# Block sums leave PSUM by another engine, a plain guard, the last store in pieces, and a new order: attention and a relu² network on one core

## The chip, the cores and the metric

The kernel runs on one core of a Trainium2 chip. Its engines have separate instruction queues: TensorE (PE) multiplies, VectorE (DVE), ScalarE (ACT) and GpSimd (POOL) do elementwise work, and SyncE (SP) issues the transfers (DMAs). SBUF is the memory on the chip that the engines work in; PSUM is the one that PE writes into and DVE and ACT can read. The metric is the device time of one execution, in microseconds; the median of three is shown. An engine works through its queue strictly in order, so an instruction that waits holds all behind it.

## What is computed

```python
k_sum = k.reshape(B, H, nb, 32, D).max(axis=3)        # B, H, S, D = 4, 8, 768, 64;  nb = 24
v_sum = v.reshape(B, H, nb, 32, D).mean(axis=3)
scores_l = scale * q @ k.T, masked to |i - j| < 16
scores_s = scale * q @ k_sum.T + log(32)
a = exp(scores - max);  a = a / (a.sum() + 1e-9)      # over both kinds of keys together
x = a @ concat(v, v_sum)                              # 3072 tokens x 512
r = maximum(x @ w_in, 0);  out = (r * r) @ w_out      # 512 -> 2048 -> 512
```

All is float32. Each query sees its neighbours within 15 places and one summary of each of the 24 blocks of its sequence.

## The kernel before

**Attention.** The queries are cut into 48 groups of 64; a group is all 8 heads of 64 positions, in four tiles of 128 rows (two heads each). A row of scores has 118 columns: 94 neighbours and 24 block summaries. Per group, in this order: PE makes the scores (L840; for the first eight groups the mask is added by a second matmul, whose left side is the constant `unscale`), DVE takes each row's maximum (L933) and scales it (L937), ACT takes the exps and sums them (L978), DVE adds 1e-9 to the sums (L990) and inverts them (L993), DVE multiplies the rows by the inverse (L999), PE transposes them (L1028), ACT copies the transposed tile out (L1035), and PE multiplies by the values (L1099) to give `att`, the x of the network. x is then split into a high part (`xh`, ACT L1156) and a rest (`xl`, DVE L1159), since PE multiplies at full rate only in a shorter format; each product of the network is the sum of three terms (high·high, high·rest, rest·high).

The mean values of the blocks of the first batch are made by PE (`vps`) and copied out of PSUM by the task `VS0` (L674): four copies of 24 rows and 128 columns into `fv_lent`. POOL copies them from there into the value tiles of the first eight groups (L795). The maxima of keys are taken by DVE (L595), four to a batch.

**The network.** 3072 tokens are six units of 512. The first two are done plainly: for each of 16 column blocks f of 128, `h` = x·w_in (L1296, twelve matmuls of 512 columns), relu, square and split (ACT L1305, L1306, L1309, DVE L1312), then `o` += g·w_out (L1322, twelve matmuls). The first two blocks of the first unit are done in halves of 256 tokens, called 0a, 1a, 0b, 1b, since only four groups are ready at first. The weights come as 64-bit words and are turned into high and rest by ACT (L1222, L1239) and DVE (L1225, L1231, L1246), one tile per block, in the time of the first unit. The other four units are done in two stages of products of sums of quarters (Strassen's scheme): L1837 and L1620 on PE. Of the last stage's last product the sums are added to `u` by DVE in two halves (L1566), each stored by a transfer (L1559).

**What sets the order.** Each piece of work is a task with an engine, a cost and a due time (`add` of the class `Plan`). `Plan.order` simulates the engines: whenever an engine comes free it takes the ready task with the earliest due time. The instructions of each engine are then issued in the order that it found. So the tables of due times (`SUMS_AT`, `VISITS`, `COMBS`, and `NUDGE`, which shifts single tasks) and the costs only set the order; the hardware runs each queue in that order, and waits by semaphores.

## Times and profile before

| | |
|---|---|
| median of 3 runs | 568.62 us (567.89, 568.62, 568.65) |
| profiled execution | 567.89 us |
| its span | 566.1 us (1.8 us lie around it) |
| PE busy | 556.9 us, 98% |
| DVE, ACT, POOL busy | 83%, 66%, 6% |
| chain that ended last | PE 93%, DVE 4%, DMA 1%, ACT 1% |
| granted clock of PE | full in all slices |

The span is the stretch that the profiler's trace covers. Busy is the time in which an engine runs something; the share of the whole span is an average over stages that have different limits, so the section of rows below cuts it into stretches. The chain is followed back from the last instruction, at each step to what released it. A row of the timeline has the idle time of its engine ahead of it in brackets, with what ended it.

### The profile page before, as it was taken

To read this page: it belongs to the slowest core of one execution; us is meant where nothing else is said; L and a number is where in the kernel's file an instruction comes from. 1 tells how busy PE (TensorE), PEld (TensorE's weight loads), DVE (VectorE), ACT (ScalarE), POOL (GpSimd) and SP (SyncE) were. 2 spreads that over 40 slices of the span, in tenths; PEclk is the share of its full clock that TensorE was granted. 3 is DMA by queue.
4 is the path that set the end of the run, shared out by engine and by line. 5 is a ranking of instruction groups with operands and counts; after the bars stand their busy time and mean duration, and the time that the engine had idled before them with its cause. 6 is when DMAs were issued, how large, how long until landed. Compare 5 with 4: busy or idle time off the path is not lost.

```text
span 566.1 us, 11857 instructions
## 1 busy us (share of the span) xinstructions
PE 556.9 (98%) x3952; PEld 458.7 (81%) x3952; DVE 471.0 (83%) x1190; ACT 373.9 (66%) x968; POOL 36.3 (6%) x88
## 2 busy tenths in 40 slices
PE   8899999999999999999999999999999999999996
PEld 7688888888888888888888888888888888888885
DVE  5999999989799998999978889997493466868863
ACT  3899799778877887786336688847375532554441
POOL 5400000012001130000000200000000000000000
PEclk9999999999999999999999999999999999999999
DMA  8998999999999999899877989897975677767682
GB/s 303 348 372 319 350 316 375 302 335 330 361 301 317 329 334 358 291 298 400 279 226 230 293 246 290 273 281 232 303 210 161 190 196 193 190 199 230 196 228 91
DMA packets 86810, 156.75 MB, mean 277 GB/s; under 512 B 8996, under 2 KB 30566, under 8 KB 86750
## 3 DMA queue, kind: packets, MB, share of 16 engines
q1 hardware_dynamic: 85597, 152.95, 83.2%
q0 software_dynamic: 1152, 3.05, 3.2%
q8 instruction: 32, 0.52, 0.4%
q14 instruction: 29, 0.23, 0.1%
HBM read 111.66 MB, written 47.94 MB: 282 GB/s over the span
## 4 chain that ended last, share of the span: by engine, by line
PE 93%; DVE 4%; DMA 1%; ACT 1%; SPq 0%; issue 0%; DVEq 0%
PE o L1620 23%; PE o L1322 16%; PE h L1296 15%; PE o L1837 14%; PE sz L1837 8%; PE x L1099 4%; PE att L1620 4%; PE att L840 3%; PE sa L1837 3%; PE att L1837 2%; DMA kb<-kT 1%; DVE small L933 1%; PE t L1028 1%; DVE qvpa_lent L999 1%; ACT qvpa_lent L978 1%; DVE kb L595 0%
## 5 line engine op out<-in xcount | busy, mean ns | idle before, releaser
L1602 ACT CAST gh<-g 128x512 fp32r<-128x512 f32 x112 | 69.2, 621 | 53.1 <-PE o L1620 22.7
L1620 PE MATMUL o<-gh,w 128*128 128x512 f32 x384 | 103.3, 391 | 0.0
L1607 DVE TENSOR_TENSOR gl<-g,gh 128x512 fp32r<-128x512 f32 x112 | 76.1, 686 | 21.1 <-ACT gh L1602 19.9
L1620 PEld LDWEIGHTS o<-gh,w 128*128 128x128 f32 x384 | 71.7, 188 | 15.0
L1296 PE MATMUL h<-xh,w 128*128 128x512 f32 x240 | 74.5, 392 | 0.0
L1874 ACT ACTIVATE g<-g 128x512 f32<-128x512 f32 x60 | 37.8, 632 | 49.4 <-DVE g L1870 49.3
L1322 PE MATMUL o<-w,gh 128*128 128x512 f32 x240 | 62.3, 396 | 0.0
L978 ACT ACTIVATE p<-p,small 128x118 f32<-128x118 f32 x160 | 61.5, 389 | 0.3 <-DVE small L915 0.2
L1620 PE MATMUL o<-gl,w 128*128 128x512 f32 x192 | 59.2, 390 | 0.0
L1296 PEld LDWEIGHTS h<-xh,w 128*128 128x128 f32 x240 | 44.7, 188 | 9.5 <-ACT rl_0b L1305 0.2
L1322 PEld LDWEIGHTS o<-w,gh 128*128 128x128 f32 x240 | 44.2, 188 | 9.3 <-ACT rl L1306 0.2
L1296 PE MATMUL h<-xl,w 128*128 128x512 f32 x120 | 46.8, 390 | 0.0
L1620 PEld LDWEIGHTS o<-gl,w 128*128 128x128 f32 x192 | 36.0, 188 | 7.5
L1837 PE MATMUL o<-w,w 128*128 128x512 f32 x160 | 40.5, 389 | 0.0
L1837 PEld LDWEIGHTS o<-w,w 128*128 128x128 f32 x160 | 30.0, 188 | 6.2
L915 DVE CUSTOM_DVE_ANT_0 p<-att,mask 128x118 f32<-128x118 f32 x152 | 33.0, 276 | 2.1 <-PE att L840 2.0
L1837 PE MATMUL sz<-xh,w 128*128 128x512 f32 x128 | 34.3, 390 | 0.0
L1322 PE MATMUL o<-w,gl 128*128 128x512 f32 x120 | 33.6, 390 | 0.0
L1597 DVE TENSOR_TENSOR g<-g 128x512 f32<-128x512 f32 x48 | 32.7, 686 | 0.2
L1870 DVE CUSTOM_DVE_ANT_0 g<-sz,g 128x512 f32<-128x512 f32 x32 | 22.0, 687 | 12.0 <-ACT g L1857 6.9
L978 ACT ACTIVATION_READ_ACCUMULATOR p<-p,small 128x1 f32 x160 | 30.8, 193 | 0.0
L1837 PE MATMUL o<-xh,w 128*128 128x512 f32 x112 | 30.1, 391 | 0.0
(197 smaller groups left out, 1092.3 us busy)
## 6 DMA issues: line engine op xcount, KB each, us to landing
raw<-wW SPq DMA_DIRECT2D x32, 512.0 KB, 8.1
w<-scr_t SPq DMA_DIRECT2D x64, 256.0 KB, 2.8
w<-scr_s SPq DMA_DIRECT2D x64, 256.0 KB, 3.1
w<-scr_a SPq DMA_DIRECT2D x48, 256.0 KB, 3.2
w<-scr_i SPq DMA_DIRECT2D x44, 256.0 KB, 3.1
turn<-a SPq DMA_DIRECT2D x17, 512.0 KB, 4.2
scr_t<-ci SPq DMA_DIRECT2D x16, 512.0 KB, 6.7
v<-vS SPq DMA_DIRECT2D x34, 192.0 KB, 3.4
```

What stands on the lines that cost most here:

```text
L915: nc.vector.tensor_tensor_reduce(out=pr.tile[:, j, :KEYS], in0=score_at(g, 0, j), in1=mask_of(g)[0], scale=-SCALE, scalar=-NEG, op0=ALU.ad ...
L978: nc.scalar.activation(x, score_tile(g, p % parts)[:, p] if by_pe else x, AF.Exp, bias=nm.tile[:, p : p + 1], scale=SCALE if by_pe else -1 ...
L1099: nc.tensor.matmul(x_of(i)[h % 2 * D : (h % 2 + 1) * D, h // 2, :], lhsT=v_bufs[g].tile[:KEYS, h * D : (h + 1) * D], rhs=av[:KEYS, 2 * c : ...
L1296: nc.tensor.matmul(cut(h), lhsT=lhs.tile[:, k // 2, k % 2 * P : (k % 2 + 1) * P], rhs=rhs[:, k, c0 : c0 + n], start=(i == 0), stop=(i == 3 ...
L1322: nc.tensor.matmul(o_of(o, t).rearrange("p (h c) -> p h c", h=2), lhsT=terms[i][0].tile[:, (t - t0) * P : (t - t0 + 1) * P], rhs=terms[i][ ...
L1597: lambda x=x, ins=ins, op=op: nc.vector.tensor_tensor(out=x.tile, in0=ins[0].tile, in1=ins[1].tile, op=op),
L1602: f"GH{s}_{n}", "ACT", 0.54, lambda x=x, gh=gh: nc.scalar.copy(out=gh.tile, in_=x.tile), due - GH_LEAD, ready,
L1607: lambda x=x, gh=gh, gl=gl: nc.vector.tensor_tensor(out=gl.tile, in0=x.tile, in1=gh.tile.bitcast(F32), op=ALU.subtract),
L1620: nc.tensor.matmul(o.tile[:, d], lhsT=chunk.tile[:, w * HALF + d * P : w * HALF + (d + 1) * P], rhs=y.tile, start=begins and w == 0 and y ...
L1837: nc.tensor.matmul(o.tile, lhsT=lhs(w, k), rhs=y[k], start=begins and i == 0, stop=i == 5, skip_group_check=not begins,)
L1870: lambda: nc.vector._custom_dve(TENSOR_ADD_SAT, out=to.tile, in0=o.tile, in1=x.tile, s0=HUGE, s1=0.0), key, deps,
L1874: f"G{name}_{s}", "ACT", 0.57, lambda: nc.scalar.activation(to.tile, to.tile, AF.Square), key + 0.7, [t], use=[to]
```

## The change

- The four copies of `VS0` are done by ACT in place of DVE.
- The guard (adding 1e-9) was a tensor-scalar instruction with two operations and an accumulator that is read by a second instruction; it is now one plain addition. The planner's cost for it is lower, and it counts it among the instructions that can hold or be held by POOL (`LOCKS`).
- The last product of all is made in three groups of matmuls: the first 128 rows of it whole, the other 128 by columns 0 to 255 and 256 to 511. Each has its own sum and its own store.
- The left side of the mask term is the identity matrix in place of `unscale`. The possibility to scale q ahead is added but not used (`Q_SCALED_BY` is eight dashes).
- The masks beyond the second are due later on POOL.
- All tables of due times are new, so every queue is in another order.

```diff
-FIRST_LS = -32.673
+FIRST_LS = -186.491
...
+FIRST_SUMS_BY = 'A'
...
-SUMS_AT = (50.909, 101.7, 156.402)
+SUMS_AT = (52.647, 93.76, 176.523)
...
-        d = at[1]
+        d, c = at[1], at[2] if len(at) > 2 else slice(None)
         if isinstance(d, int):
-            return self.bufs[d].tile
+            return self.bufs[d].tile[:, c]
         assert d.stop == d.start + 1
-        return self.bufs[d.start].tile.unsqueeze(1)
+        return self.bufs[d.start].tile[:, c].unsqueeze(1)
...
         def gather():
             for c in range(ns):
-                nc.vector.tensor_copy(out=vs.tile[:NB, c * DM // ns : (c + 1) * DM // ns], in_=out_ps.tile[c * SQ : c * SQ + NB, : DM // ns])
+                (nc.vector.tensor_copy if FIRST_SUMS_BY == "D" else nc.scalar.copy)(
+                    out=vs.tile[:NB, c * DM // ns : (c + 1) * DM // ns], in_=out_ps.tile[c * SQ : c * SQ + NB, : DM // ns]
+                )
...
-                            lhsT=q_bufs[g].tile[rows, p, :] if term else unscale[rows, :],
+                            lhsT=q_bufs[g].tile[rows, p, :] if term else unscale[rows, :] if g in t_QS else ident[rows, rows],
...
-        nm = buf("nm", 3, (P, 3 * NPAIR + 1), F32, f"nm{g}")
+        nm = buf("nm", 3, (P, 3 * NPAIR), F32, f"nm{g}")
...
-            nc.vector.tensor_scalar(
-                out=rec, in0=den, scalar1=1e-9, scalar2=0.0, op0=ALU.add, op1=ALU.add, accum_out=nm.tile[:, 3 * NPAIR : 3 * NPAIR + 1]
-            )
+            nc.vector.tensor_scalar_add(rec, den, 1e-9)
             nc.vector.reciprocal(out=rec, in_=rec)
...
-            for i, piece in enumerate((todo[::2], todo[1::2]) if end else (todo,)):
+            whole = slice(0, TU)
+            pieces = [(todo, whole)]
+            if end:
+                pieces = [(todo[::2], whole), (todo[1::2], slice(0, TU // 2)), (todo[1::2], slice(TU // 2, TU))]
+            for i, (piece, c) in enumerate(pieces):
...
-                    d = slice(i, i + 1)
-                    t = plus("C12", u2, o, u2, due + 2, [t_p, made["U2"]], d=d)
-                    leave(f"12_{s}_{i}", u2, 0, 1, due + 3, [t], d)
+                    d = slice(i > 0, 1 + (i > 0))
+                    t = plus("C12", u2, o, u2, due + 2 + 0.1 * i, [t_p, made["U2"]], d=d, c=c)
+                    leave(f"12_{s}_{i}", u2, 0, 1, due + 3 + 0.1 * i, [t], d, c)
```

The lines of the changed kernel have numbers up to 19 higher than those of before: L674 stays, L933 is L952, L937 is L956, L978 is L991, L990 is L1003, L999 is L1010, L1035 is L1046, L1296 is L1307, L1322 is L1333.

First place: DVE's queue where the copies of the block sums stood. `small` holds the maxima, sums and inverses of a group (three buffers in turn), `o` are scores in PSUM, `qvpa_lent` rows after the exps. Before:

```order
L999 TENSOR_TENSOR qvpa_lent<-qvpa_lent,small_85 128x4x118
L674 COPY fv_lent<-vps_325 24x128 x4
L990 TENSOR_SCALAR small_86<-small_86 128x4
L993 RECIPROCAL small_86<-small_86 128x4
L933 TENSOR_REDUCE small_72<-o_66 128x4
L937 TENSOR_SCALAR small_72<-small_72 128x4
```

The same place now:

```order
L1010 TENSOR_TENSOR qvpa_lent<-qvpa_lent,small_85 128x4x118
L952 TENSOR_REDUCE small_72<-o_66 128x4
L956 TENSOR_SCALAR small_72<-small_72 128x4
L1003 TENSOR_SCALAR small_86<-small_86 128x4
L1004 RECIPROCAL small_86<-small_86 128x4
L1010 TENSOR_TENSOR qvpa_lent<-qvpa_lent,small_86 128x4x118
```

The copies are gone, and the maximum of the next group (number 3) stands ahead of the guard.

Second place: ACT's queue at the exps of that group (`small_72`) and of the next. Before:

```order
L1035 COPY qvpa_lent<-t_421 128x4x4x32
L978 ACTIVATE qvpa_lent,small_72<-o_66,small_72 128x118 x4
L1035 COPY qvpa_lent<-t_456 128x4x4x32
L978 ACTIVATE qvpa_lent,small_85<-o_67,small_85 128x118 x4
L1156 CAST xh<-att_68 128x4x64
L1035 COPY qvpa_lent<-t_510 128x4x4x32
```

And now:

```order
L1046 COPY qvpa_lent<-t_406 128x4x4x32
L991 ACTIVATE qvpa_lent,small_72<-o_66,small_72 128x118 x4
L674 COPY fv_lent<-vps_323 24x128 x4
L1046 COPY qvpa_lent<-t_451 128x4x4x32
L991 ACTIVATE qvpa_lent,small_85<-o_67,small_85 128x118 x4
L1046 COPY qvpa_lent<-t_495 128x4x4x32
```

The four copies stand between the exps of the group and the copy of a transposed tile; the cast of x, which stood ahead of the last row, comes later.

Third place: PE's queue at the third column block, `h_2`. `gh_0a` and `gl_0a` are the high part and the rest of block 0 for the first half of the tokens, `gh_1a` and `gl_1a` those of block 1. Before:

```order
L1322 MATMUL o_67<-w_0_624,gh_0a 128x512 x2
L1322 MATMUL o_67<-w_0_624,gl_0a 128x512
L1296 MATMUL h_2_855<-xh,w_2_807 128x512 x2
L1296 MATMUL h_2_855<-xl,w_2_807 128x512
...
L1322 MATMUL o_67<-w_1_724,gh_1a 128x512 x4
L1322 MATMUL o_67<-w_1_724,gl_1a 128x512 x2
```

And now:

```order
L1333 MATMUL o_67<-w_1_704,gh_1a 128x512 x4
L1333 MATMUL o_67<-w_1_704,gl_1a 128x512 x2
L1307 MATMUL h_1b<-xh,w_1_716 128x256 x2
L1307 MATMUL h_1b<-xl,w_1_716 128x256
...
L1307 MATMUL h_2_870<-xh,w_2_829 128x512 x2
L1307 MATMUL h_2_870<-xl,w_2_829 128x512
```

The six matmuls of block 1's first half stood behind `h_2` and stand now ahead of it, and ahead of `h_1b` too.

## Rows read from the trace of the kernel before

**Rows 1.** Busy time by stretch: PE, PEld, DVE, ACT, POOL; PEclk, DMA share, GB/s

```profile
10.00:40.45 30.45, 27.23 (x532) 22.34 (x531) 28.57 (x93) 27.04 (x102) 7.87 (x23) 1.00 0.99 361
40.45:561.56 521.11, 521.11 (x3362) 428.30 (x3360) 437.52 (x1092) 344.55 (x863) 22.19 (x31) 1.00 0.87 274
561.56:566.10 4.54, 0.00 (x0) 0.00 (x0) 0.73 (x2) 0.00 (x0) 0.00 (x0) 0.94 0.32 116
```

**Rows 2.** Waits of PE: who, for whom, us in total, times, longest

```profile
PE t L1028 <- DVE qvpa_lent L999: 2.4, 4, 0.9
```

**Rows 3.** Chain of waits, 0 to 46 us: start, length, what

```profile
17.57 0.29 DVE fv_lent L674
...
19.06 1.47 ACT qvpa_lent L978 x8
...
20.88 1.51 ACT qvpa_lent L978 x8
```

**Rows 4.** Timeline of DVE, 14 to 26 us: start, length, instruction

```profile
16.69 1.17 DVE L674 COPY fv_lent<-vps 24x128 f32<-24x128 f32 x4
17.79 0.14 DVE L990 TENSOR_SCALAR_CACHE_REDUCE small<-small 128x4 f32<-128x4 f32 x1
...
18.86 0.17 DVE L937 TENSOR_SCALAR small<-small 128x4 f32<-128x4 f32 x1
...
20.17 0.46 DVE L937 TENSOR_SCALAR small<-small 128x4 f32<-128x4 f32 x1
```

**Rows 5.** Groups of ACT's instructions by form: busy us, mean ns | idle before

```profile
L1156 ACT CAST xh<-att 128x256 fp32r<-128x256 f32 x8 | 2.9, 387 | 0.0
L864 ACT COPY kw<-kb 128x96 f32<-128x96 f32 x19 | 5.3, 278 | 6.2 <-DVE kb L595 5.6 <-POOL kb L853 0.5
```

**Rows 6.** Timeline of ACT, 14 to 26 us

```profile
19.06 0.36 ACT L978 ACTIVATE qvpa_lent<-o,small 128x118 f32<-128x118 f32 x1 [0.64 <-DVE small L937]
...
22.88 0.58 ACT L1035 COPY qvpa_lent<-t 128x512 f32<-128x512 f32 x1 [0.24 <-PE t L1028]
```

**Rows 7.** Chain of waits, the second half product of block 1

```profile
44.83 1.36 PE o L1322 x6
```

**Rows 8.** Timeline of PE, 33 to 47 us

```profile
41.84 0.71 PE L1296 MATMUL h<-xh,w 128*128 128x512 f32 x2
```

**Rows 9.** Timeline of DVE, 38 to 78 us

```profile
41.10 0.66 DVE L1246 TENSOR_TENSOR w<-t,w 128x512 fp32r<-128x512 f32 x1
...
63.09 1.80 DVE L595 TENSOR_REDUCE kb<-kb 128x24 f32<-128x768 f32 x2
...
71.30 1.18 DVE L1246 TENSOR_TENSOR w<-t,w 128x1024 fp32r<-128x1024 f32 x1
```

**Rows 10.** Timeline of POOL, 16 to 34 us

```profile
18.94 1.66 POOL L795 COPY qvpa_lent<-fv_lent 24x512 f32<-24x512 f32 x2
```

**Rows 11.** Line 990: count, duration ns min/median/max, first and last start us

```profile
L990 DVE TENSOR_SCALAR_CACHE_REDUCE small<-small x48: 114/151/158, 12.7 to 393.0; 128x4 f32<-128x4 f32 x48
```

**Rows 12.** Timeline of DVE, 558 to 567 us

```profile
560.92 1.37 DVE L1566 TENSOR_TENSOR u<-att,u 128x512 f32<-128x512 f32 x2 [2.50 <-PE att L1620]
```

**Rows 13.** Chain of waits, 256 columns: an elementwise piece, and twelve matmuls

```profile
24.08 0.33 DVE xl L1159
...
39.17 1.44 PE h_1b L1296 x12
```

**Rows 14.** Timeline of SP, 560 to 567 us

```profile
561.64 1.01 SPq L1559 DMA_DIRECT2D out<-u  x2
```

**Rows 15.** DMA queue, 562 to 566 us: packets, MB, share of 16 engines

```profile
q1 hardware_dynamic: 288, 0.52, 36.7%
```

**Rows 16.** Timeline of SP, 54 to 58 us

```profile
54.87 2.17 SPq L592 DMA_DIRECT2D kb<-kT  x4
```

**Rows 17.** Chain of waits, the first load of keys

```profile
2.20 6.21 DMA kb<-kT
```

**Rows 18.** Timeline of PE, 72 to 77 us

```profile
75.00 0.62 PE L1296 MATMUL h<-xh,w 128*128 128x512 f32 x2
```

More of the change, by code (lines that the diff above doesn't have):

```diff
@@ L548, in attention_then_relu2_ffn @@
     t_mask = {
-        off: add(f"mask{off}", "POOL", 1.45, lambda off=off: make_mask(off), -99 + 3 * i)
+        off: add(f"mask{off}", "POOL", 1.45, lambda off=off: make_mask(off), -99 + 3 * i if i < 2 else -20)
         for i, off in enumerate(masks)
@@ L673, in gather @@
             for c in range(ns):
-                nc.vector.tensor_copy(out=vs.tile[:NB, c * DM // ns : (c + 1) * DM // ns], in_=out_ps.tile[c * SQ : c * SQ + NB, : DM // ns])
+                (nc.vector.tensor_copy if FIRST_SUMS_BY == "D" else nc.scalar.copy)(
+                    out=vs.tile[:NB, c * DM // ns : (c + 1) * DM // ns], in_=out_ps.tile[c * SQ : c * SQ + NB, : DM // ns]
+                )
         own = len(tail) % 4 == 0
-        t_VS[0] = [add("VS0", "DVE", 0.85, gather, -53, [last], take=[vs] * own, use=[out_ps] + [vs] * (not own))]
+        t_VS[0] = [add("VS0", "DVE" if FIRST_SUMS_BY == "D" else "ACT", 0.85, gather, -53, [last], take=[vs] * own, use=[out_ps] + [vs] * (not own))]
     scr_v = {
@@ L871, in keys_of @@
         b, w = divmod(g, NW)
-        return [t_QL[g]] + ([t_KC[g - 1]] if w else [t_K[b][p] for p in pairs])
+        return [t_QS.get(g, t_QL[g])] + ([t_KC[g - 1]] if w else [t_K[b][p] for p in pairs])
     def first_attention(g):
@@ L880, in first_attention @@
         by_pe = g < PE_MASKS
+        if Q_SCALED_BY[g : g + 1] in ("A", "P"):
+            scaled_q(g)
         s_bufs[g] = [o_buf(f"s{g}_{i}") for i in range(len(parts))]
@@ L885, in first_attention, with scaled_q, scale @@
                 f"S{g}_{i}", "PE", (0.97 if by_pe else 0.5) / len(parts) + 0.07 * (len(parts) > 1), lambda i=i, pairs=pairs: scores(g, pairs, by_pe, i),
-                due - 15, keys_of(g, pairs) + [t_unscale, mask_of(g)[1]] * by_pe, take=[s_bufs[g][i]], use=[q_bufs[g]],
+                due - 15, keys_of(g, pairs) + [t_unscale, t_ident, mask_of(g)[1]] * by_pe, take=[s_bufs[g][i]], use=[q_bufs[g]],
             ))
         softmax(g, by_pe)
+    t_QS = {}
+    def scaled_q(g):
+        q = q_bufs[g]
+        by_act = Q_SCALED_BY[g] == "A"
+        def scale():
+            if by_act:
+                nc.scalar.activation(q.tile, q.tile, AF.Copy, scale=SCALE)
+            else:
+                nc.gpsimd.tensor_scalar(out=q.tile, in0=q.tile, scalar1=SCALE, scalar2=None, op0=ALU.mult)
+        t_QS[g] = add(f"QS{g}", "ACT" if by_act else "POOL", 0.36 if by_act else 0.8, scale, wanted(g) - 30, [t_QL[g]], use=[q])
     def softmax(g, by_pe=False):
@@ L937, in most @@
                     nc.vector.tensor_scalar_mul(m, m, SCALE)
-            def scale(js=js):
-                m = nm.tile[:, :NPAIR][:, js]
-                nc.gpsimd.tensor_scalar(out=m, in0=m, scalar1=SCALE, scalar2=None, op0=ALU.mult)
             if not by_pe:
@@ L949, in softmax @@
                 ))
-                if scaled:
-                    t_x[-1] = add(f"XC{name}", "POOL", 0.25, scale, due - 12.95, [t_x[-1]], use=[nm])
             def less(i=i, js=js, nj=nj):
@@ L1558, in leave, with plus @@
             add(
-                f"PS{name}", "SP", 0.42, lambda: nc.sync.dma_start(out=rows[:, d], in_=by_two(x)[:, d]), due, deps, use=[x],
-                size=(d.stop - d.start) * 4 * P * DM, begin=due - 20,
+                f"PS{name}", "SP", 0.42, lambda: nc.sync.dma_start(out=rows[:, d, c], in_=by_two(x)[:, d, c]), due, deps, use=[x],
+                size=(d.stop - d.start) * (c.stop - c.start) * 4 * P, begin=due - 20,
             )
-        def plus(name, to, o, x, key, deps, take=(), d=slice(0, 2)):
+        def plus(name, to, o, x, key, deps, take=(), d=slice(0, 2), c=slice(0, TU)):
             made[name] = add(
-                f"{name}_{s}_{d.start}", "DVE", 0.08 + 0.54 * (d.stop - d.start),
-                lambda: nc.vector.tensor_tensor(out=by_two(to)[:, d], in0=o.tile[:, d], in1=by_two(x)[:, d], op=ALU.add),
+                f"{name}_{s}_{d.start}" + "b" * (c.start > 0), "DVE", 0.08 + 0.54 * (d.stop - d.start) * (c.stop - c.start) / TU,
+                lambda: nc.vector.tensor_tensor(out=by_two(to)[:, d, c], in0=o.tile[:, d, c], in1=by_two(x)[:, d, c], op=ALU.add),
                 key, deps, take=take, use=[o, x] + [to] * (not take),
```

56 lines of the change are left out of this document (28 added, 28 removed), and 7 rows, old and new, of the table NUDGE.

## The prediction

> **What bounds the kernel now.** I read the windows first. The reader is to see two lives of TensorE in them [rows 1]. From 40.45 to 561.56 us its busy time is the whole stretch, 521.11 of 521.11: nothing that makes DVE, ACT or a transfer faster there can move the end, and only fewer or shorter matmuls could; the change takes no matmul away. From 10 to 40.45 it is busy 27.23 of 30.45, so 3.22 us are idle. After 561.56 come 4.54 us with no matmul at all: the last sums, the last store and its landing. All that a new order can win is therefore in those 3.22 us and in the tail, and all it can lose is a gap opened in a stretch that has none.
>
> The list of waits says who causes the 3.22: the transposes of the softmaxed rows wait for the normalizing multiply of DVE, 2.4 us in four waits [rows 2]. The chain of waits of the first 40 us agrees: it runs through DVE and ACT there, and the four small copies of the block sums stand in it, then the exps of ACT [rows 3]. So in that stretch DVE and ACT are a series, and what leaves it counts in full, until something else is late.
>
> **The sums to ACT.** DVE's queue loses the four 24x128 copies: they start at 16.69 and the next instruction starts at 17.79, 1.10 us [rows 4]. ACT gets them. No row shows ACT copying 24x128 out of PSUM. The nearest are 128x96 from SBUF at 278 ns and 128x256 from PSUM at 387 ns [rows 5]; The eight instructions of four exps take 1.47 us [rows 3], 0.18 each from start to start, and less than that none of its instructions costs; so four copies cost 0.74 to 1.55 us. I take 0.95, nearer to the smaller tile.
>
> Where they land decides. In the new order ACT does them behind the four exps of group 3 and ahead of the next transpose copy. In the trace of before ACT sat 0.64 us waiting for the maximum of that group, and began at 19.06 [rows 6]. That maximum now comes 1.10 earlier, so the exps begin at about 18.0. From there to the exps of group 4 it took 1.82 us (19.06 to 20.88, [rows 3]); with the copies 18.0 + 1.82 + 0.95 = 20.77, which is 0.11 ahead of before. Then the wait of 0.24 at 22.88 [rows 6] closes, and one cast that stood ahead of it comes behind: ACT is 0.5 to 0.9 ahead by 25 us. DVE, 1.10 ahead and then held by ACT in places, is 0.6 to 1.0 ahead. At ACT's upper price it would be about 0.5 behind at 20.77, and the gain would be nearly nothing; at the lower it is 0.25 better. The copies of the sums into their value tiles on POOL start some 2.5 us later than before, behind ACT, and are wanted by TensorE only at about 21.5: covered by half a microsecond or more.
>
> **The new order at 35 to 42 us.** What is won early has to be spent on TensorE work that was late before. The second half product of f=1 (six matmuls of 512 columns, 1.36 us [rows 7]) now stands ahead of the third FFN column block, and before it stood behind. That block starts at 41.84 [rows 8], 0.08 us after its weights are done on DVE (41.10 + 0.66 [rows 9]). Summing DVE's queue ahead of those weights in the new order, the copies (1.10) and one weight conversion less (1.14), and a guard, a transpose, half a conversion and two normalizing multiplies more (0.29 + 0.63 + 0.38 + 1.12), is +0.1 to +0.2: they are ready at about 41.9 to 42.0 again. Without the shift TensorE, with 1.36 more to do, would come to that block at 41.84 + 1.36 = 43.20; 0.6 to 1.0 ahead, it comes at 42.2 to 42.6, and the weights are not late. If it could start with them, at 41.94, the gain would be 1.26. I take 42.1, a gain of 1.1, toward the upper end: the new order also puts the transposes of later groups behind half products that are ready, where TensorE stood up to 0.9 us [rows 2].
>
> **The guard.** The add of 1e-9 loses its accumulator. In the trace it is 0.14 us plus a 0.07 read behind it; a plain tensor-scalar on the same 128x4 takes 0.17 [rows 4], and the reciprocal that follows needs its result anyway. Between a loss and a gain of a few hundredths for each of 48, and off the path after 40 us: 0. But the plain form has a row against it. The one at 18.86 took 0.17 us, the one at 20.17 took 0.46 [rows 4], and the latter lies within the span of POOL's copies from 18.94 to 20.60 [rows 10]. So the guard may now be held by 0.29 us when POOL copies, where the accumulating form took 158 ns at most in 48 [rows 11]. POOL is busy 7.87 of the 30.45 us [rows 1], about a quarter, so of eight guards some two are hit: 0 to 0.6 us, I take 0.2, already within the 1.1. The Trainium skill says the same of the mechanism (SBUF — State Buffer, "Who interferes with whom"): a plain tensor-scalar may take the port pair that VectorE shares with GpSimd and is then blocked for a whole instruction, the form that writes its accumulator may not. By that rule the sum would be worse by up to those 0.6, without it by nothing; the two rows of the plain form agree with it, and the 48 of the other too.
>
> **The last product.** The second store is split by columns. DVE's two adds take 1.37 us from 560.92 [rows 12], and they are in series: the second starts when the first lets go, not when TensorE does. Halves cost 0.33 each when queued [rows 13], 0.42 the last one, so the adds end at 560.92 + 0.68 + 0.33 + 0.42 = 562.35 where they ended at 562.29. Matmuls of 256 columns cost 0.12 each (1.44 for twelve [rows 13]), as half of 512 would. The queue of SP took 1.01 us for two issues [rows 14] and now has a third, 0.1 to 0.2 later than the second was. What it gains is that the last store is half as large: 288 packets took 36.7% of 16 engines' 4 us [rows 15], 0.08 us each, so 128 packets on 16 engines 0.65 us, and half as many bytes 0.33 to 0.65. Net -0.25 to +0.2; I take -0.1.
>
> **What else moves.** The mask term now takes the identity where it took another constant: the same matmuls, 0. The last mask on POOL is made later and read later. Beyond 75 us the order is new everywhere, but the full TensorE stretch says its inputs were early; I cost that at nothing while nothing is late, and the price of its failing is the third rival.
>
> **The sum.** -1.1 - 0.1 = -1.2 against the profiled execution's 567.89, so 566.7. That execution is the fastest of the three shown, and the median stands 0.73 above it; the median is what is predicted, so 568.62 - 1.2 = 567.4. Its own range is 566.8 to 567.9 (gain 0.7 to 1.8).
>
> **Rivals.** *Given back* (0.28). The copies cost ACT their upper price, or the guard is held twice, or TensorE waits for the weights of the next block: the startup wins 0.1 to 0.6. Time 568.2. For it: ACT is busy 27.04 of 30.45 us there [rows 1], so it has little room; against it, its waits stand just where the copies go.
>
> *The next batch's keys come late: slower* (0.18). In the new order the four maxima of the next batch's keys stand ahead of the weights of the seventh and eighth blocks on DVE. Before they began at 63.09 [rows 9]; adding up DVE's new queue with the durations of before they are wanted at about 57.7. Their loads were issued from 54.87 [rows 16] and the same load took 6.21 us at the start [rows 17], so before they were in at about 61. By the new queue of SP they stand behind a score product that TensorE ends at about 47.4, so they should be in by 54 to 55. If the queue of SP holds them as late as before, DVE stands 3.4 us, and behind it the weights; those of the eighth block were done at 72.48 (71.30 + 1.18 [rows 9]) for a matmul at 75.00 [rows 18], a margin of 2.5 that the earlier start and the moved work cut to 0.6. So TensorE idles some 2.5 us less the 1.2 won: +1.3, 569.9. It decides from a delay of 1.9 us on those loads. Against it: SP's new place for them leaves about 3 us.
>
> *More than that* (0.10). TensorE's idle of 3.22 us [rows 1] shrinks by two thirds or more because all four waits of the transposes close: -2.4, with the tail -2.6, so 566.0. Against it: DVE and ACT are busy 94% and 89% of the stretch, there is not the room.
>
> **How the numbers follow.** Forecast 0.44, given back 0.28, slower 0.18, more 0.10. About 0.2% of 568.62, 1.14 us, is what a measurement here can tell from no change; 567.4 is barely beyond it. Of the forecast's 0.44 some 0.33 falls below 567.48, the rest within; with the 0.10 of the last rival and 0.03 of the first: faster 0.46. Slower: 0.16 of the third's 0.18, and 0.03 of the others: 0.19. Within: 0.35. The range goes from 565.6 to 569.6: below it 0.07, above it 0.1.
>
> **What would show it.** Right: no DVE copy at 16 to 18 us, four copies on ACT in the stretch of 19 to 20.5 us at 0.17 to 0.39 each; TensorE's wait for the normalizing multiply falls from 2.4 to about 1.3 us; the third block's matmul starts at about 42.1 with the six moved matmuls before it; no wait on TensorE between there and the end; the last matmul about 1.1 earlier and 4.4 to 4.5 us from it to the end. Wrong: copies on ACT above 0.39; a guard over 0.3 beside a POOL copy on the path; a TensorE wait for a weight tile or for the key maxima between 55 and 80 us; a tail longer than 4.54.

## The result, and the profile after

The changed kernel takes 572.63 us (median of 16 runs, 567.6 to 575.7) against 568.28 us of the kernel before (16 runs on the same chip, 567.56 to 569.36): a ratio of the means of 1.0062, 95% interval 1.0038 to 1.0085. By the medians it is 4.35 us slower, outside the forecast range; by the means 3.5. The spread is a finding too: 8.1 us of the kernel after, 1.8 us of the one before. Of the 16 runs of after the seven of 571.02 us or less have a mean granted clock of 0.998 or 0.999, and the nine of 572.59 or more, the profiled one among them, 0.992 to 0.997: the stretch at half clock that is shown below need not be in every execution, and the median lies just above a gap.

The profiled execution of after took 572.68 us with a span of 571.0, 4.9 more than before. The page (busy us, share of the span, instructions; then the chain that ended last):

```profile
PE 559.7 (98%) x3955; PEld 460.6 (81%) x3955; DVE 468.1 (82%) x1139; ACT 373.9 (65%) x972; POOL 39.4 (7%) x88
...
PE 85%; issue 5%; DMA 3%; ACT 3%; DVE 2%; POOL 1%; SPq 0%; DVEq 0%; POOLq 0%
```

The chain was 93% PE before and is 85% now, though PE is just as busy: work of others has come onto the path. The windows of after say where (the columns are those of [rows 1]):

```profile
10.00:40.45 30.45, 27.82 (x530) 22.26 (x529) 27.47 (x86) 27.64 (x112) 8.72 (x22) 1.00 1.00 357
40.45:200.00 159.55, 159.55 (x1182) 131.02 (x1181) 149.93 (x411) 134.17 (x344) 11.16 (x15) 1.00 0.97 325
200.00:250.00 50.00, 48.02 (x421) 38.88 (x420) 41.89 (x145) 35.11 (x109) 8.21 (x9) 0.97 0.98 311
...
350.00:450.00 100.00, 99.37 (x600) 81.66 (x599) 74.27 (x154) 64.74 (x162) 0.80 (x1) 1.00 0.80 244
...
566.41:571.00 4.59, 0.00 (x0) 0.00 (x0) 0.76 (x3) 0.00 (x0) 0.00 (x0) 0.88 0.35 114
```

The long stretch that was full [rows 1] has two holes: 1.98 us idle from 200 to 250, where the granted clock also falls to 0.97, and 0.63 from 350 to 450. PE's list of waits (us in total, times, longest) answers to [rows 2]:

```profile
PE x L1110 <- POOL v L794: 1.6, 2, 1.2
...
PE o L842 <- issue: 0.9, 1, 0.9
PE t L1039 <- ACT qvpa_lent L1046: 0.8, 2, 0.4
PE t L1039 <- DVE qvpa_lent L1010: 0.8, 2, 0.6
```

The wait for DVE at the start did shrink from 2.4 to 0.8 us, though 0.8 for ACT and 0.9 with no releaser shown came in. The new one is on top: the value products wait for POOL, which divides the block sums. PE's timeline there (start, us, what, idle before and its releaser):

```profile
205.76 0.69 PE L1110 MATMUL x<-a,v 118*64 118x64 f32 x16 [0.40 <-POOL v L794]
207.69 0.83 PE L1110 MATMUL x<-a,v 118*64 118x64 f32 x16 [1.25 <-POOL v L794]
208.45 1.22 PE L1307 MATMUL h<-xh,w 128*128 128x512 f32 x2
...
212.04 0.62 PE L1307 MATMUL h<-xh,w 128*128 128x512 f32 x2
```

The same pair of matmuls takes 1.22 us right after the wait and 0.62 at 212.04. The windows of one us each show the granted clock (third column from the end):

```profile
206.00:207.00 1.00, 0.44 (x16) 0.30 (x12) 1.00 (x8) 0.34 (x1) 1.00 (x1) 1.00 1.01 185
207.00:208.00 1.00, 0.31 (x10) 0.31 (x12) 1.00 (x11) 0.00 (x0) 0.64 (x1) 1.00 0.88 217
208.00:209.00 1.00, 1.00 (x15) 0.83 (x11) 0.50 (x1) 0.44 (x2) 0.00 (x0) 0.54 1.01 312
209.00:210.00 1.00, 1.00 (x4) 0.77 (x3) 0.00 (x0) 1.00 (x6) 0.00 (x0) 0.50 1.06 372
...
211.00:212.00 1.00, 1.00 (x4) 0.80 (x4) 0.74 (x2) 1.00 (x6) 0.98 (x2) 0.75 1.07 411
```

PE was busy 0.44 and 0.31 in the two microseconds from 206, and then ran at half clock (1.2 of 2.4 GHz) until the middle of 211 (the row of 210, left out, has 0.50 too, and that of 212 has 1.00). Of the four microseconds from 208 are lost 0.46 + 0.50 + 0.50 + 0.25 = 1.7 us, as much again as the 1.65 us of waiting. Together: 1.98 idle + 1.7 slow + 0.63 idle later = 4.3 of the span's 4.9. The rest is 0.05 in the tail and small sums; at the start idle fell by 0.59, but 0.5 more went into the warm-up matmuls (8.7 to 9.2 us), so nothing was won there.

**Why POOL was late.** The values of each later batch of queries need its block sums. They are made by seven transfers in series: one plain, and six that add to what is there (these are issued by POOL, L759 before, L761 after). Each waits for the one before it to land. Batch 3's are due from the third entry of `SUMS_AT`, which the change moves from 156.402 to 176.523. POOL's timeline, after:

```profile
186.82 0.83 POOL L761 DMA_DIRECT2D scr_v<-vS  x1 [14.01 <-DMA scr_v<-vS]
...
195.38 0.81 POOL L761 DMA_DIRECT2D scr_v<-vS  x1 [7.36 <-DMA scr_v<-vS]
203.27 0.80 POOL L761 DMA_DIRECT2D scr_v<-vS  x1 [7.09 <-DMA scr_v<-vS]
204.15 3.49 POOL L794 TENSOR_SCALAR v<-v 24x512 f32<-24x512 f32 x2
```

And before:

```profile
168.06 0.83 POOL L759 DMA_DIRECT2D scr_v<-vS  x1 [24.01 <-DMA scr_v<-vS]
...
182.99 0.80 POOL L759 DMA_DIRECT2D scr_v<-vS  x1 [5.82 <-DMA scr_v<-vS]
...
190.60 0.80 POOL L759 DMA_DIRECT2D scr_v<-scr_v  x1 [6.43 <-DMA scr_v<-vS]
196.85 3.23 POOL L792 TENSOR_SCALAR v<-v 24x512 f32<-24x512 f32 x2 [5.46 <-DMA v<-scr_v]
```

The first accumulating transfer of batch 3 comes 18.8 us later (168.06, 186.82). So it is now its third that stands ahead of the two divisions of batch 2's values, and POOL, in order, waits 7.09 us for a landing that those divisions have no use for. They end at 207.6; before they ended at 200.1, and PE came to x at 202.55, without a wait:

```profile
202.55 1.15 PE L1099 MATMUL x<-a,v 118*64 118x64 f32 x32
```

The margin was 2.5 us.

**A second thing, on SP.** The attention rows of some groups are turned by a store to memory and four fetches of it (L1083 and L1088 after; L1072 and L1077 before). SP's timeline, after and then before:

```profile
196.29 0.35 SPq L1083 DMA_DIRECT2D turn<-a  x1
196.74 0.40 SPq L1507 DMA_DIRECT2D scr_t<-ci  x1
204.04 1.70 SPq L1088 DMA_DIRECT2D a<-turn  x4
```

```profile
197.06 0.32 SPq L1072 DMA_DIRECT2D turn<-a  x1
197.42 0.44 SPq L1823 DMA_DIRECT2D w<-scr_i  x1
197.90 1.27 SPq L1438 DMA_DIRECT2D scr_a<-w  x2
...
201.74 1.20 SPq L1077 DMA_DIRECT2D a<-turn  x1
```

After, the fetches stand almost directly behind the store, and SP issues nothing from 197.1 to 204.0. Before, five others were issued meanwhile. Over the whole execution SP's waits for turned stores go from 8.1 us in five to 18.1 in six.

### The profile page after: what moved, and what is told of

The parts are those of the page before. It is cut to its first block, busy times and chain, and to the rows that moved or that the text cites. A ratio compares the mean times of both kernels' runs of the same rounds, so it can differ in the third digit from the quotient of the medians.

```text
span 571.0 us, 11800 instructions
## 1 busy us (share of the span) xinstructions
PE 559.7 (98%) x3955; PEld 460.6 (81%) x3955; DVE 468.1 (82%) x1139; ACT 373.9 (65%) x972; POOL 39.4 (7%) x88
## 4 chain that ended last, share of the span: by engine, by line
PE 85%; issue 5%; DMA 3%; ACT 3%; DVE 2%; POOL 1%; SPq 0%; DVEq 0%; POOLq 0%
PE o L1631 23%; PE o L1852 14%; PE h L1307 11%; PE o L1333 11%; PE sz L1852 8%; PE att L1631 4%; PE x L1110 3%; PE sa L1852 3%; PE att L842 3%; PE att L1852 2%; PE warm L559 2%; DMA scr_v<-vS 1%; DMA scr_s<-cr 1%; ACT qvpa_lent L991 1%; PE t L1039 1%
## 5 line engine op out<-in xcount | busy, mean ns | idle before, releaser
L1307 PE MATMUL h<-xh,w 128*128 128x512 f32 x240 | 75.7, 397 | 0.0
L991 ACT ACTIVATE p<-p,small 128x118 f32<-128x118 f32 x160 | 61.5, 390 | 6.8 <-DVE small L934 6.7
L1333 PE MATMUL o<-w,gh 128*128 128x512 f32 x240 | 62.0, 394 | 0.0
L1307 PEld LDWEIGHTS h<-xh,w 128*128 128x128 f32 x240 | 45.3, 191 | 9.5
L1333 PEld LDWEIGHTS o<-w,gh 128*128 128x128 f32 x240 | 44.3, 188 | 9.3
L1307 PE MATMUL h<-xl,w 128*128 128x512 f32 x120 | 47.3, 394 | 0.0
L1333 PE MATMUL o<-w,gl 128*128 128x512 f32 x120 | 33.6, 389 | 0.0
L991 ACT ACTIVATION_READ_ACCUMULATOR p<-p,small 128x1 f32 x160 | 31.0, 194 | 0.0
```

Of the source, the lines that this page charges most:

```text
L991: nc.scalar.activation(x, score_tile(g, p % parts)[:, p] if by_pe else x, AF.Exp, bias=nm.tile[:, p : p + 1], scale=(1.0 if scaled else SC ...
L1307: nc.tensor.matmul(cut(h), lhsT=lhs.tile[:, k // 2, k % 2 * P : (k % 2 + 1) * P], rhs=rhs[:, k, c0 : c0 + n], start=(i == 0), stop=(i == 3 ...
L1333: nc.tensor.matmul(o_of(o, t).rearrange("p (h c) -> p h c", h=2), lhsT=terms[i][0].tile[:, (t - t0) * P : (t - t0 + 1) * P], rhs=terms[i][ ...
```

## The experiments

The theory with which they began: the order, not the edits, costs the time; in the order it is the late block sums, through POOL. The rival: the edits, or the order in many small places. Each time below stands beside the kernel before on the same chip; the ratios are of the means. A profile is of one execution, and not always of one near the median.

**1. The divisions ahead of the third accumulating transfer** (new order, one task moved by hand on POOL):

```diff
+        t = todo.pop(names.index("FS3_3"))
+        todo.insert([t.name for t in todo].index("LD25") + 1, t)
```

`todo` is the order that the planner found, `FS3_3` the transfer and `LD25` the second of the divisions.

> The changed kernel with one instruction moved on POOL: the third accumulating transfer of batch 3's sums (L761) is issued behind the two divisions of batch 2's values (L794) instead of ahead of them; all other queues are as in the changed kernel. Theory 1 (POOL's queue): the third transfer waits on POOL until the second has landed, and the divisions stand behind it; TensorE waits 1.65 us for them at 205 us and then runs at half clock for some 3 us. Then both waits vanish, the clock stays at full in 200 to 250 us, and the profile is 3.4 us shorter: 569.0 to 569.4 us where the changed kernel has 572.6, with a spread between runs like that of before (2 us, not 8). Theory 2 (the value rows are late by themselves, since the loads moved on SP): the x product waits still, 572 us or more, spread as it was.

Measured 572.39 us (571.75 to 572.96, 4 runs), before 568.19; ratio 1.0077 (1.0064 to 1.0090). Nothing came back. PE's wait for POOL is gone (x ran at 204.79 without one), but from 217.7 us there is this:

```profile
219.78 0.64 PE L842 MATMUL att<-kw,q 64*64 64x118 f32 x16 [2.06 <-DMA q<-qW]
```

A load of q is late instead, and the granted clock behind that wait is 0.50 again (222 to 224 us). So POOL's queue is where the lateness shows in after's profile, and not its source; my theory in that form fell.

**2. The same stretch with PE kept busy** (new order, the scores of the visit at 204 us made three times, 64 matmuls more, with the same values):

```diff
+            for _ in range(2 * (both[-1:] == [25] or tuple(both[-1:]) == (25,))):
+                for g in then:
+                    scores(g, range(NPAIR), False)
```

> The changed kernel with the scores of the visit at 204 us made three times instead of once (64 matmuls more, 1.94 us by the 0.97 of one such set), ahead of the x product that waits. POOL's queue is untouched, so the divisions end at about 207.65 as before. Theory 1a (TensorE's clock falls because it stands idle there): no idle time of 1.65 us any more in the runs that waited up to 1.9 us, granted clock full through 205 to 215 us, profile 1.6 us shorter although work was added: about 571.0. Theory 1b (the clock falls for another reason, the time of the program or the power drawn): the clock still falls to 0.5 after 208 us, and the time is 572.6 or more.

Measured 571.68 us (570.01 to 573.16, 6 runs), before 568.19. The window of 200 to 250:

```profile
200.00:250.00 50.00, 47.86 (x483) 39.03 (x483) 39.91 (x141) 33.85 (x106) 7.51 (x9) 1.00 0.98 304
```

The waits for POOL are still there, 0.32 and 0.87 us (0.40 and 1.25 in after), with 0.94 for ACT at 245; yet the clock stayed at 1.00 and no matmul ran at half rate. All six runs have a mean clock of 0.998 to 1.0. So the half clock is no price of the order as such; it goes with what PE does around the wait. Whether the shorter waits or the 64 matmuls kept it up was not taken apart: in the two microseconds from 207 PE was busy 0.68 and 0.13, hardly more than the 0.44 and 0.31 of after. In time nothing was gained that can be told. The 64 matmuls cost 1.6 us (205.31 to about 206.9), as much as the full clock gives back; the profiled execution took 573.16 us, after's 572.68, where about 571.0 was expected, and the medians, 0.95 apart, differ by less than the runs scatter.

**3. The order before with two more transfers ahead of the divisions** (the fifth and sixth accumulating transfers moved up on POOL):

```diff
+        t = todo.pop(names.index("FS3_5"))
+        todo.insert([t.name for t in todo].index("FS3_4") + 1, t)
+        t = todo.pop([t.name for t in todo].index("FS3_6"))
+        todo.insert([t.name for t in todo].index("FS3_5") + 1, t)
```

> The kernel before with the same fault put in: the fifth and sixth accumulating transfers of batch 3 (one POOL copy of keys moves with them, behind) are issued ahead of the two divisions of batch 2's values. Theory 1: the sixth waits for the fifth to land at about 204.5, the divisions end at about 208.3, TensorE, which wants them from 202.5, idles 4 to 5.5 us and then runs at half clock for 3 us or more: 568.3 + 5.5 to 7.5 = 574 to 576 us, and the spread between runs grows to some 4 us or more. Theory 2 (order on POOL does not matter, the values are late for another reason in the changed kernel): within 0.5 us of 568.3.

Measured 576.23 us (575.5 to 576.88, 4 runs), before 568.19; ratio 1.0141 (1.0127 to 1.0156). As expected, PE waits for POOL, and the clock falls in the same window (0.90 from 200 to 250 us, 0.50 around the late x); the time is 0.23 above the expected 574 to 576, and the wider spread that was expected did not come (1.4 us).

```profile
PE x L1099 <- POOL v L792: 6.0, 2, 5.6
```

The mechanism on POOL is real and costs several us where it decides. In after it is one of several things that come late together.

**4 and 5. The edits without the order.** In the order before: the four copies on ACT alone; then copies, plain guard and three stores together.

```diff
-                nc.vector.tensor_copy(out=vs.tile[:NB, c * DM // ns : (c + 1) * DM // ns], in_=out_ps.tile[c * SQ : c * SQ + NB, : DM // ns])
+                nc.scalar.copy(out=vs.tile[:NB, c * DM // ns : (c + 1) * DM // ns], in_=out_ps.tile[c * SQ : c * SQ + NB, : DM // ns])
```

> The kernel before with the four copies of the first block sums on ACT in place of DVE, at the place that the planner's order gives them; nothing else moved. By the prediction's sum the copies cost ACT 0.95 (in the profile of the changed kernel they took 1.05), and DVE gains 1.10; the start of the exps of group 3 comes earlier, but the order of TensorE is the old one, so the weights of the third block (0.08 us of margin) bound it: 0 to -0.9 us, 567.4 to 568.3. A rival (copies on ACT hold the exps and the transposed tile behind them): +0.3 to +1.0.

> The kernel before, its order kept in every queue, with the three edits that are not due times: the four copies of block sums on ACT, the plain guard, the last product in three pieces. By the prediction: copies 0 to -0.9 with this order, guard 0 to +0.6, pieces -0.25 to +0.2: 567.3 to 568.6, the likeliest 567.9, so no change that can be told. Tail from the end of the last matmul 4.4 to 4.5 us against 4.54. A rival (the edits are what makes the changed kernel slow): 570 or more.

Measured 567.62 us (ten runs from 567.34 to 568.56; an eleventh took 693.09, at a mean granted clock of 0.754 where the ten have 0.998 to 1.0) against 568.19, ratio of the ten 0.9994 (0.9985 to 1.0003); and 567.96 (567.54 to 569.29, 11 runs) against 567.99, ratio 0.9999 (0.9989 to 1.0008). In this order the edits are worth nothing that can be measured, in either direction. The identity under the mask and the later masks are in neither run, and were not tried alone. With the copies on ACT, PE's waits at the start are these:

```profile
PE o L840 <- DMA qvpa_lent<-qW: 0.8, 1, 0.8
PE t L1028 <- ACT xh L1156: 0.7, 1, 0.7
PE o L840 <- issue: 0.6, 1, 0.6
PE t L1028 <- DVE qvpa_lent L999: 0.6, 2, 0.4
```

DVE's 2.4 us became 0.6, and 2.1 us of other waits took its place. The startup's gain went into the next thing that was late.

**6 and 7. The one number.** The third entry of `SUMS_AT`, put back in the new order and put in alone in the old one:

```diff
 # new order
-SUMS_AT = (52.647, 93.76, 176.523)
+SUMS_AT = (52.647, 93.76, 156.402)
 # order before
-SUMS_AT = (50.909, 101.7, 156.402)
+SUMS_AT = (50.909, 101.7, 176.523)
```

> The changed kernel with one number put back: the due time of batch 3's sums (the third of SUMS_AT) is 156.4 again in place of 176.5; the planner then starts those seven transfers some 20 us earlier, and few other places of the queues move (40 of TensorE's rows). What is left out of it is the shift alone. Theory A (the late sums are the root: they hold POOL's divisions, and their traffic, each transfer reading and adding 384 KB, also delays the loads of q at 211 us): neither wait, full clock in 200 to 250 us, 568.3 to 569.3. Theory B (two separate faults; the loads of q stand too late on SP in the new order): no wait for the divisions, but 1.5 to 2.5 us for q at about 217.5 and half clock behind it, 571.5 to 572.5 as in the run with the divisions first.

> The kernel before with the mirror edit: the third of SUMS_AT is 176.5 in place of 156.4. TensorE's queue is the same but for a few rows; on POOL the second accumulating transfer now stands ahead of the divisions, the third behind them; on SP the loads of q keep their early place ahead of the w loads. Theory A: the later traffic alone delays loads: +1 to +4 us. Theory B: the divisions have to wait only for the second transfer's issue, the q loads are early: within 0.5 us of before, 567.7 to 568.8.

Measured 570.83 us in the new order (569.28 to 572.66, 6 runs; before 567.99, ratio 1.0051, 1.0036 to 1.0067) and 571.23 in the old (569.78 to 573.0, 6 runs; ratio 1.0057, 1.0042 to 1.0072). This number alone costs the old order 3.2 us. PE's waits there, from 200 us on:

```profile
PE x L1099 <- ACT g L1857: 1.2, 1, 1.2
PE att L840 <- DMA q<-qW: 1.0, 1, 1.0
PE o L1837 <- ACT os L1359: 0.9, 1, 0.9
```

No wait for POOL among them. From 170 to 180 us the 16 engines were busy 0.85 at 277 GB/s there, and 0.79 at 268 GB/s in after, where the kernel before has 1.08 at 322: the first of the seven transfers are taken out of that stretch, and the series runs on into one where others are due. On the chain that leads to the last of the three waits one transfer (`scr_s<-cs`, issued at 200.26) took 10.32 us; its like in experiment 11 took 6.23. What comes late then differs from case to case. Putting the number back in the new order recovers 1.5 us by the medians (4.35 to 2.84 above before) and 0.6 by the means, which is not clear of the scatter of after: the two intervals overlap. It is not all in any case.

**8. Two loads on SP behind the values' load, with edit 1:**

```diff
+        t = todo.pop([t.name for t in todo].index("FS3_3"))
+        todo.insert([t.name for t in todo].index("LD25") + 1, t)
+        t = todo.pop([t.name for t in todo].index("QL32"))
+        todo.insert([t.name for t in todo].index("V25") + 1, t)
+        t = todo.pop([t.name for t in todo].index("QL31"))
+        todo.insert([t.name for t in todo].index("V25") + 1, t)
```

> The changed kernel with both queues mended by hand and nothing else: on POOL the third accumulating transfer behind the two divisions, on SP the two q loads of the visit at 217 us issued right behind the visit at 204 us, ahead of four stores and loads of weights. Theory B: they land some 4 to 5 us earlier, neither wait is left, full clock in 200 to 250 us; the profile of the run with the divisions first less its 2.06 us wait and the 1.7 us of half clock: 568.6 to 569.2, spread 2 us. Theory A: the transfers are late with the traffic; the q loads land only 1 to 2 us earlier, a wait of 0.5 to 1.5 us stays or a third load comes late: 570 to 572.

Measured 572.28 us (571.49 to 573.81, 5 runs), before 567.99. Nothing came back; the wait only moved, to the load of the values:

```profile
PE x L1110 <- DMA v<-vS: 3.1, 1, 3.1
```

From 200 to 205 us the 16 engines were busy only 0.60. They had room, and SP was not giving them work: that led to the next three.

**9 to 11. The four fetches of the turned tile on SP.** In the new order put behind the load of q that followed them: first with edit 1, and then with the number of 6 in that one's place; and the reverse in the order before, where the fetches go right behind their store:

```diff
 # new order
+        t = todo.pop([t.name for t in todo].index("TR27_3"))
+        todo.insert([t.name for t in todo].index("QL31") + 1, t)
...
 # order before
+        t = todo.pop([t.name for t in todo].index("TR27_3"))
+        todo.insert([t.name for t in todo].index("TW27") + 1, t)
...
```

The same two lines follow for `TR27_2`, `TR27_1` and `TR27_0`; `TW27` is the store.

> The changed kernel with two places moved by hand: on POOL the third accumulating transfer behind the divisions (as in the first run), and on SP the four loads of the turned tile of groups 26 and 27 (L1088) behind the two stores, the two loads of weights and the q load that stood behind them. Theory C (in the new order these loads stand right behind the store that they read back, so SP issues nothing for 7 us from 197 to 204, and the transfer engines run empty: share 0.6 to 0.8 where before had 0.98): the share of 200 to 205 us rises to 0.9 or more, q and v land 3 to 5 us earlier, no wait over 0.5 us at 217 us, full clock: 568.6 to 569.8. Theory A alone (the late sums): the wait for a load stays at 1.5 us or more, 571 to 573.

> The changed kernel with the due time of batch 3's sums put back to 156.4 and the same four loads moved on SP. Theories A and C together: no wait on TensorE from 45 us on but small ones, full clock throughout, share of 200 to 205 us at 0.95: 568.0 to 568.8, as before, with a spread of 2 us. If the remaining 2.8 us of the run with the sums put back have other causes (due times of weights and x after 250 us): 570 to 571.

> The kernel before with the mirror move on SP alone: the four loads of the turned tile of groups 26 and 27 right behind the store that they read back, ahead of seven other transfers. Theory C: SP stands from 197.5 to about 202, the share of the transfer engines falls from 0.98 to 0.8 in those 5 us; before's q and v loads have about 2 us in hand, so a wait of 0 to 2 us near 215: 568.3 to 570.5, with more spread. A rival (SP's wait is harmless, transfers already issued fill the time): 567.7 to 568.5, share unchanged.

Measured, in this order: 571.29 us (567.89 to 572.98, 8 runs; before 568.41, ratio 1.0041, 1.0021 to 1.0061); 569.46 (567.06 to 571.59, 12 runs; ratio 1.0017, 1.0002 to 1.0033); 570.52 (569.22 to 572.15, 8 runs; ratio 1.0035, 1.0021 to 1.0048). The first two missed what the theory of SP's queue gave for them (568.6 to 569.8, and 568.0 to 568.8); the third is at the upper end of its range. The windows of 200 to 205 us (last columns: clock, share of the DMA engines, GB/s), first of the second kernel, then of the third (executions of 568.53 us, and of 572.15, the slowest of its eight):

```profile
200.00:205.00 5.00, 5.00 (x57) 3.91 (x58) 4.93 (x12) 2.90 (x5) 2.80 (x2) 1.00 1.05 401
```

```profile
200.00:205.00 5.00, 5.00 (x78) 4.01 (x77) 5.00 (x16) 3.29 (x9) 3.00 (x5) 1.00 0.40 109
```

With the fetches moved back SP issues from 199.60 on and the transfer engines are full; with them moved up in the order before SP stands from 197.15 to 202.59, the engines are empty more than half of the time, and what was full for PE before has a wait of 1.9 us (for ACT at L1359, until 245.72). The chain that ends in that wait goes back through DVE and ACT to this transfer, issued behind the fetches:

```profile
207.13 6.23 DMA scr_s<-cs
```

Both directions agree: an SP queue that stands behind one landing costs 1.4 us in the new order (570.83 to 569.46 on one chip; 1.8 when each is taken from the kernel before that ran with it; the two intervals do not overlap) and 2.1 in the old. Number and fetches together take back 3.3 of the 4.35 us, by the means 2.6 of 3.5.

**12. Copies back on DVE in the new order, with the number of 6:**

```diff
-                (nc.vector.tensor_copy if FIRST_SUMS_BY == "D" else nc.scalar.copy)(
+                nc.vector.tensor_copy(
```

> The changed kernel with the sums put back to 156.4 and the four copies of the first block sums on DVE again, at the same place of the order; to be compared with the run with the sums put back alone (570.83). By the prediction's step (the copies on ACT win 1.1 us): 571.6 to 572.2. By the profiles after it (what DVE no longer holds, loads of q and a gap in the scores hold: 0.6 to 1.1 us): 570.6 to 571.3; the third block starts at 43.2 to 43.6 instead of 42.6 to 43.4.

Measured 570.67 us (569.64 to 572.33, 6 runs) where the same with copies on ACT had 570.83: no difference in the new order either. In its one profile the third block starts at 43.66, behind the 42.61 to 43.40 of the seven profiles of the new order with the copies on ACT; if that is a gain of the copies, nothing of it is left at the end.

**13 to 15. All fetches of turned tiles later**, by the planner's allowance for a transfer behind a store: in the new order with the number of 6, in the new order alone, and in the order before.

```diff
-TURN_LATE = 0.4
+TURN_LATE = 3.4
```

> The new order with the block sums of batch 3 begun at 156.4 as before, and with the planner's allowance for a transfer that follows a store raised from 0.4 to 3.4 us, so that the fetches of every turned tile stand later in SP's queue and others stand ahead of them. Theory (what is left of the loss is SP standing with its queue behind stores that it reads back): SP's waits for turned tiles fall well below the 18 to 20 us of the new order, and the time comes to 568.0 to 568.6, with a spread of 2 us or less. Rival (the third turned tile was the only one that mattered, the rest is the new order's own small stalls in many places): 569.0 to 570.0, like the run with only that tile moved, 569.46. Second rival (an order with other allowances moves the stalls to places not looked at): 570 or more.

> The new order with the allowance for a transfer behind a store at 3.4 us, the block sums of batch 3 left at 176.5. Theory that the late sums cost some 1.8 us and SP's standing the rest: 570 to 571.5, a part of the 4.35 us taken back. Rival that SP's standing is the whole cause and the late sums act only through it: 568 to 569. Rival that SP's standing costs only beside the early sums: 572 to 573, no change.

> The order before with the allowance at 3.4 us alone: the fetches of the turned tiles stand later there too. Theory (before already has its transfers early enough, so there is nothing to win): 567.6 to 568.6. Rival (SP's waits of 8.1 us for turned tiles cost something in before too): below 567.5. Rival (any replanned order loses): above 569.

Measured 584.3 us (582.91 to 587.56), 580.28 (579.94 to 583.68) and 586.4 (585.49 to 588.88), 5 runs each, before 568.29. All three missed; of what I had put down only the rivals of a replanned order that loses elsewhere held. SP's longest wait for a turned store did fall, to 2.4 us, but the planner put a whole attention visit late: the twelfth of the visits' value products ran at 242.01 in the kernel before, and at 266.76 in the first of these. The chain of casts and differences behind it has nothing beside it:

```profile
273.37 5.37 PE L1852 MATMUL o<-w,w 128*128 128x512 f32 x12 [5.46 <-ACT w L1725]
```

Twelve matmuls took 5.37 us where they take 2.88 in the kernel before: after 5.46 us of standing the granted clock is 0.50 from 273 to 276. The three runs say how dear a new order can be; on the question for which they ran, whether SP's other standing is the last 1.05 us, they say nothing. That stays open.

## Why the prediction was wrong

**The step that failed** is this one: "Beyond 75 us the order is new everywhere, but the full TensorE stretch says its inputs were early; I cost that at nothing while nothing is late". A busy PE says that its inputs were early, and not by how much. The margin at 202.55 us was 2.5 us, and it could be read: the divisions ended at 200.1, with a transfer of the next batch on either side of them on POOL. The moved table entry stood in the diff, 20 us on a series of seven transfers that follow each other 6 to 10 us apart. My slower rival looked for the late input in the first 80 us, at the keys of the next batch; there PE stayed full (40.45 to 200 us, above), and it did not occur. The price for that kind of failure, +2.5 less the gain, was too small as well, since a wait of this size brought a stretch at half clock with it. Its own sum gives more, too: 3.4 us of standing less a margin of 0.6 is 2.8. (In the startup's sum the copies at ACT's lower price are 0.21 us better than at 0.95, not 0.25; that decides nothing.)

**The startup, -1.1: not there.** The four copies left DVE as said. On ACT, and then on PE:

```profile
19.67 1.05 ACT L674 COPY fv_lent<-vps 24x128 f32<-24x128 f32 x4
20.74 0.59 ACT L1046 COPY qvpa_lent<-t 128x512 f32<-128x512 f32 x1
...
21.37 0.63 PE L1039 MATMUL t<-ident,qvpa_lent 128*128 128x128 f32 x4 [0.43 <-ACT qvpa_lent L1046]
...
43.25 0.63 PE L1307 MATMUL h<-xh,w 128*128 128x512 f32 x2
```

They cost 1.05 us for four (0.95 taken, bounds 0.74 to 1.55). But the exps ahead of them began at 18.32, where I had 18.0, and the next group's at 21.22, where I had 20.77 and before has 20.88: ACT was 0.34 behind there and not 0.11 ahead. The copy of the transposed tile behind the four held PE 0.43 us at 21.37. The third block starts at 43.25, with 1.36 us of moved matmuls ahead of it: comparable to 41.89, where [rows 8] have 41.84. I expected it at 42.1, where 43.20 meant no gain; it came at 43.25. Over seven profiles of the new order with the copies on ACT that start, less 1.36, lies between 41.25 and 42.04 (mean 41.63), and over six of the order before between 41.45 and 41.95 (mean 41.74). DVE's wait shrank by 1.6 us, more than my 1.1, but ACT's 0.8 and, in four of the seven, a stall of 0.7 to 1.1 us in the scores of a group at about 24 us (no releaser shown, or a load of q) ate it: a wait that did not show in the profile of before, and that I had not priced. That is the rival "given back": in part by its own route, through ACT, in part by another.

**The guard: right at nothing, wrong at 0.2.** All 48 took 127 to 236 ns, median 164, where the accumulating form had a median of 151 and a second instruction behind it [rows 11]. On DVE's timeline one lies within a copy of POOL (12.51 to 13.10 us), and one of another task does:

```profile
12.88 0.23 DVE L1003 TENSOR_SCALAR small<-small 128x4 f32<-128x4 f32 x1
...
21.81 0.46 DVE L956 TENSOR_SCALAR small<-small 128x4 f32<-128x4 f32 x1
```

The guard lost 0.07 there, and ended as the copy did (13.11 and 13.10); the scaling of the maximum lost 0.29, as its like did before [rows 4]. I had two guards of eight held by 0.29 each; the copies fell elsewhere. The Trainium skill (SBUF — State Buffer, "Who interferes with whom") has a plain tensor-scalar as one that GpSimd can hold; L956 agrees, and so do the guards: the longest of all runs, 0.36 us at 12.78 in experiment 5, lies beside a copy of POOL too (12.63 to 12.99).

**The tail: -0.1 expected, +0.05 measured.** Three adds and three issues:

```profile
565.72 1.47 DVE L1577 TENSOR_TENSOR u<-att,u 128x512 f32<-128x512 f32 x3 [2.50 <-PE att L1631]
...
566.44 1.31 SPq L1570 DMA_DIRECT2D out<-u  x3
```

They answer to 1.37 us for two adds [rows 12] and 1.01 for two issues [rows 14]. From the last matmul to the end of the issues it is 1.34 us (566.41 to 567.75) where it was 1.09 (561.56 to 562.65), and from there to the end of the span 3.25 where it was 3.45: the smaller last store won 0.20, within the 0 to 0.33 that my sum left it (0.33 to 0.65 us in place of 0.65), while the adds cost 0.05 more and the third issue 0.20, where I had 0.06 and 0.1 to 0.2. Each term is inside its bounds, and so is the sum (-0.25 to +0.2). The Trainium skill (DMA: Bandwidth & Descriptors, "Anatomy of one DMA — SWDGE (gpsimd) path") puts most of a small transfer's time into a fixed part of about 2 us, mostly for the confirmation of its landing, for transfers of GpSimd's path. For this store, which SP issues, the trace agrees in kind: half the bytes took 0.20 of 3.45 us away.

## What to carry to other kernels

A stretch in which the bounding engine is always busy has no loss, but it has margins; before a new order is costed at nothing there, read for each series of dependent transfers when it ends and when it is wanted, and look in the diff for the entries that move it. Ask of every in-order queue what stands behind an instruction that waits for a landing: a transfer that reads back a store belongs behind other issues, not behind the store. And test single entries of a replanned table, both ways: here one number of the table cost 3.2 us by itself in the order before, and the edits nothing there.

## What the runs showed of the hardware

- Standing can cost twice. After 1.65 us of waits within 2.4 us PE ran at half clock for over three us (1.7 us lost); with waits of 1.19 us in the same place and 64 matmuls more around them the clock stayed full. A wait of 2.06 us (experiment 1) and one of 5.60 (experiment 3) were followed by half clock too, and one of 1.90 (experiment 11) from 247 to 250 us; after three waits of 1.18, 0.99 and 0.86 us that ended at 235.14, 243.48 and 246.06 (experiment 7, old order) the clock stayed full.
- In after an accumulating transfer of batch 3 stood 4.5 to 7.4 us on POOL for the landing of the one before it, and in before 5.8 and 6.4, while the transfer engines were nearly full (share 1.02 to 1.06 from 188 to 204 and from 210 to 224 us of after). From the first such issue of batch 3 to its sixth it is 38.4 us before (168.06 to 206.42) and 37.3 after: the series moved as a whole.
- From the issue of the same turned store to the first fetch of it went 4.4 us in before (197.38 to 201.74, at most this), 5.4 in experiment 11 and 7.4 in after.
- Times can scatter where transfers come late: 16 runs of before lie within 1.8 us, 16 of after within 8.1, with the same instructions each time. It is not so each time: the four runs of experiment 3, with the longest wait, lie within 1.4.
